# Transposed scores for the first two attention tiles, in a fused attention, gated FFN and expert kernel

## Chip, cores and metric

One core of one Trainium2 chip runs the whole program. The metric is device time in microseconds (us) of one execution; 788.37 us is the median of three runs of the kernel before (788.2 to 789.08).

## What is computed

Three stages follow each other: windowed attention, a gated FFN, and a mixture of eight experts with one expert per token. Cut to what matters here:

```python
scores = scale * np.matmul(q, k.transpose(0, 1, 3, 2))       # 4 x 8 heads, 576 tokens, 64 wide
mask = (rel >= 0) & (rel < 64)
scores = np.where(mask, scores, -1000000000.0)
scores = scores - np.max(scores, axis=-1, keepdims=True)
attn = np.exp(scores)
attn = attn / (np.sum(attn, axis=-1, keepdims=True) + 1e-09)
x = np.matmul(attn, v)
xn = x / np.sqrt(np.mean(x * x, axis=-1, keepdims=True) + 1e-06) * rms_g
g = xn @ w_gate
x = (g * (1.0 / (1.0 + np.exp(-g))) * (xn @ w_val)) @ w_out
out[token] = gate * eom * (np.maximum(x @ w1[e], 0.0) @ w2[e])   # e = argmax of x @ gate
```

The 2304 tokens are 18 tiles of 128. The FFN is 512 to 1536 and back, the experts 512 to 1024 and back. Large products are made of three single-pass products of split operands (high with high, high with low, low with high).

## The kernel before

**Attention of a tile** is `attention_tile` (L667 to L888). Two PSUM banks hold the scores of four heads each. `mmc` forms them: four bf16 matmuls write the mask (L691), 24 f32 matmuls of 64 rows and 64 columns of the array add the products (L699). VectorE takes the largest value of a row (`mx`, L743), ScalarE scales it (`mxs`, L775) and makes the exponentials with four instructions for four heads (`ex`, L782), each with its own bias and its own row sum. TensorE transposes the probabilities (`pt`, L796), VectorE or ScalarE copies them out of PSUM (L454, L458), and TensorE multiplies them with the values (`pv`, L830). Then come the division by the sum (`guard` L810, `rc` L815, `xr` L464), the squares (L843), the norm (L848, L853, L856), a transposition (`turn`, L873) and the split into high and low parts (L454, L461).

**FFN** (`ffn_group`, `ffn_step`): for each of 12 slices of the hidden layer, 12 matmuls for the gate and 12 for the value (`gv`, L1033 to L1035), then 12 back (`mo`, L1074 to L1076). Four tiles make the first group, and its first `gv` needs all four. The weights of each slice are brought from 64 to 32 bits and split on VectorE and ScalarE during the first group. Routing (L1142, L1149, L1157), scattering and the experts (L1508 to L1741) follow.

**A branch that is already there.** With `t < K["st"]` (`turned_too`), a tile takes another way, which the kernel before never takes since `st` is 0 there. `mmt_` forms the scores a second time with keys and queries exchanged, so transposed, beside `mmc`. `less` adds the negated largest value to every column with a matmul whose stationary operand is that value spread over 128 columns and whose moving operand is the identity. One exponential over four heads writes the transposed probabilities, and `total_` makes the row sums with matmuls by a vector of ones (the lines are those of the kernel before, one more in the changed one):

```python
# L750 to L765
for i in range(4):
    nc.tensor.matmul(
        bt.t[:, i * P:(i + 1) * P], lhsT=mb.t[:, 4 * hf + i:4 * hf + i + 1].to_broadcast([P, P]),
        rhs=ident.t, start=False, stop=(i == 3),
    )
...
nc.scalar.activation(out=pb.t, in_=bt.t.rearrange("p (i t) -> p i t", t=P), func=AF.Exp, scale=scale)
...
nc.tensor.matmul(sm.t[:, at:at + 2], lhsT=pb.t[:, i], rhs=ones.t, start=True, stop=True)
...
pl.op({"t": 0.9}, less, r=[(mb, hf), ident], w=[bt], prio=ps_, rows=0.5)
pl.op({"a": 0.55}, ext, r=[bt], w=[pb], prio=ps_)
pl.op({"t": 0.45}, total_, r=[pb, ones], w=[(sm, hf)], prio=pr + 5 * sg + 0.1 * hf, rows=0.05)
```

All of these are f32 and stand once per half of a tile; `mmt_` (L714 and L724) stands once per tile.

**What sets the order.** Nothing is issued in the order of the source. `Plan.order` goes through all operations before the program is built, with a cost for each on each engine (as the 0.45 above, in us), a due time, and a correction of that due time from the table `SHIFT`. It gives each operation an engine, a place in that engine's order, and the buffer that is free first by its own reckoning. The numbers in `K` set due times, buffer counts and such. Where it sees TensorE without work in the beginning, `filled` puts in pairs of bf16 matmuls that no one reads (`fill`, L625), up to the time `K["warm"]`. Each engine then runs its instructions strictly in that order, and waits where an operand or a buffer is not ready. All loads are on SyncE's queue (SP): queries, keys and values at L660, weights at L898.

Of the kernel before, what the change touches and what calls it, by code (L numbers as in the profile page):

```python
# [35 lines left out]
TICK, FULL = 3.4133, 1.275  # L36
LAT = {"t": 0.17, "a": 0.15, "v": 0.15, "p": 0.12, "s": 0.2}
K = dict(
    w_r=4, sl=1.2, n_q=4, n_kt=4, n_s=4, n_m=4, n_p=4, n_x=4, n_xf=1, n_val=3, pf=0.1, cold=6.0, late=1, f0=24.0, pw=110.0, pb=0.6, c1a=0, c1v=0, st=0, lact=0, warm=51.238, wf=21.971, flead=24.233, nwv=1, port=1.0, t0=46.214, pp=93.267,
    lead=1.781, clead=9.978, stag=2.552, stage=1.001, slack=0.083, nt=2, look=0.033, marg=-0.474, dw=1.368, ewl=3.278,  # L40
    ews=8.339, xld=43.407, xtn=7.222, mlead=14.712, vb=0.137, vb2=0.687, tb=30.293, share=-0.016, pls=9, phs=9, sf=0, hfs=1.431, stk=-0.032, rlead=7.936, span=0.317, wl=1.841,
)


SHIFT = [
# [40 lines left out]
]  # L86


class Buf:


    def __init__(self, tag=None, t=None, like=None):
        self.tag, self.t, self.slot, self.like = tag, t, None, like
        self.last_w, self.reads = {}, {}
        self.users = 0
        self.left, self.end = 0, 0.0
        self.before = None
# [1819 lines left out]
```

## Time and profile before

| | |
|---|---|
| median of 3 runs | 788.37 us |
| the profiled execution | 788.36 us, its span 786.6 us |
| TensorE busy | 778.0 us (99%), 5712 matmul records |
| VectorE, ScalarE busy | 394.1 us (50%), 349.5 us (44%) |
| mean granted TensorE clock | 0.998 |
| DMA | 135 MB, mean 172 GB/s |

Matmuls overlap in the pipeline. So a matmul's own duration is longer than what it adds to the time; what it adds is read from the start of one group of rows to the start of the next. An f32 matmul that isn't a transposition or a split product leaves two records. "Idle before" an instruction is time in which its engine did nothing, and the arrow names what ended it.

### The profile page before, as it was taken

The numbers are of one execution on the slowest core, as the hardware profiler recorded it, in microseconds if no ns is written. First come the engines' busy times: TensorE is split into PE (matmuls) and PEld (weight loads), VectorE is DVE, ScalarE is ACT, GpSimd is POOL, SyncE is SP. The second block draws the span as 40 slices with busy tenths as digits, with TensorE's granted clock in tenths as the row PEclk, the third lists the DMA queues.
The fourth block names the chain that finished last, engine by engine and source line by source line (L and its number), as shares of the span: only waits on it lengthen the run. The fifth ranks groups of instructions, "written<-read, shape, count | busy, mean of one in ns | idle before, by whom it ended". The sixth has DMA issues, their size and how long they took to land.

```text
span 786.6 us, 14688 instructions
## 1 busy us (share of the span) xinstructions
PE 778.0 (99%) x5712; PEld 663.8 (84%) x5712; DVE 394.1 (50%) x915; ACT 349.5 (44%) x938; POOL 56.0 (7%) x108
## 2 busy tenths in 40 slices
PE   8999999999999999999999999999999999999996
PEld 7988888888888888888888888899989998999883
DVE  5988988464323226332253422258445656656500
ACT  6988788472213335411351211424344553554411
POOL 1000000002000002000002000020100011111010
PEclk9999999999999999999999999999999999999999
DMA  7888898965421027231024740274194466675511
GB/s 259 291 293 307 280 330 279 302 215 184 147 108 68 28 108 229 81 111 51 1 108 161 267 161 0 102 261 148 49 323 169 140 201 212 174 257 188 182 32 69
DMA packets 51131, 135.17 MB, mean 172 GB/s; under 512 B 6052, under 2 KB 6052, under 8 KB 51060
## 3 DMA queue, kind: packets, MB, share of 16 engines
q1 hardware_dynamic: 48052, 124.68, 47.0%
q0 software_dynamic: 3008, 9.54, 3.2%
q8 instruction: 45, 0.74, 0.4%
q14 instruction: 26, 0.21, 0.1%
HBM read 109.97 MB, written 24.23 MB: 171 GB/s over the span
## 4 chain that ended last, share of the span: by engine, by line
PE 95%; issue 3%; DMA 1%; POOLq 0%; SPq 0%; POOL 0%; ACT 0%; DVE 0%
PE bank L1033 13%; PE bank L1035 13%; PE bank L1034 13%; PE bank L1074 6%; PE bank L1075 6%; PE bank L1076 6%; PE bank L1578 4%; PE bank L1579 4%; PE bank L1580 4%; PE bank L1739 3%; PE bank L1740 3%; PE bank L1741 3%; PE bank L830 2%; PE bank L796 2%; PE bank L699 2%
## 5 line engine op out<-in xcount | busy, mean ns | idle before, releaser
L1033 PE MATMUL bank<-xn,w 128*128 128x512 f32 (+1 forms) x480 | 181.3, 378 | 0.0
L1035 PE MATMUL bank<-xn,w 128*128 128x512 f32 (+1 forms) x480 | 177.0, 369 | 0.0
L1034 PE MATMUL bank<-xn,w 128*128 128x512 f32 (+1 forms) x480 | 176.8, 368 | 0.0
L1033 PEld LDWEIGHTS bank<-xn,w 128*128 128x128 f32 x480 | 90.3, 188 | 15.7 <-PE bank L1149 0.4
L1035 PEld LDWEIGHTS bank<-xn,w 128*128 128x128 f32 x480 | 90.2, 188 | 15.7
L1034 PEld LDWEIGHTS bank<-xn,w 128*128 128x128 f32 x480 | 90.5, 189 | 14.4
L1050 DVE SCALAR_TENSOR_TENSOR u<-u,bank 128x512 f32<-128x512 f32 (+1 forms) x60 | 37.9, 632 | 115.4 <-ACT u L1045 115.3
L1074 PE MATMUL bank<-wo,h 128*128 128x512 f32 x216 | 85.3, 395 | 0.0
L1075 PE MATMUL bank<-wo,h 128*128 128x512 f32 x216 | 84.2, 390 | 0.0
L1076 PE MATMUL bank<-wo,h 128*128 128x512 f32 x216 | 84.2, 390 | 0.0
L1045 ACT ACTIVATE u<-bank 128x512 f32<-128x512 f32 (+1 forms) x60 | 33.4, 556 | 102.1 <-PE bank L1035 99.0
L461 DVE TENSOR_TENSOR w<-raw,w 128x512 fp32r<-128x512 f32 x112 | 72.0, 687 | 5.9 <-ACT w L454 5.5
L454 ACT CAST h<-u 128x512 fp32r<-128x512 f32 (+1 forms) x54 | 31.0, 574 | 93.5 <-DVE u L1058 93.5
L1058 DVE TENSOR_TENSOR u<-u,bank 128x512 f32<-128x512 f32 (+1 forms) x60 | 38.0, 633 | 65.6 <-PE bank L1035 61.4
L454 ACT CAST w<-raw 128x512 fp32r<-128x512 f32 x86 | 49.1, 621 | 23.2 <-PE bank L1741 8.7
L1578 PE MATMUL bank<-xT,w 128*128 128x240 f32 (+4 forms) x192 | 58.2, 303 | 0.0
L1579 PE MATMUL bank<-xT,w 128*128 128x240 f32 (+4 forms) x192 | 57.7, 300 | 0.0
L1580 PE MATMUL bank<-xT,w 128*128 128x240 f32 (+4 forms) x192 | 57.7, 300 | 0.0
L782 ACT ACTIVATE s<-bank,m 128x128 f32<-128x128 f32 x144 | 50.7, 369 | 0.6
L461 DVE TENSOR_TENSOR h<-u,h 128x512 fp32r<-128x512 f32 (+1 forms) x60 | 38.2, 636 | 21.8 <-ACT h L454 21.5
L1589 DVE SCALAR_TENSOR_TENSOR eh<-bank,eh 128x240 fp32r<-128x240 f32 (+5 forms) x56 | 25.4, 459 | 46.4 <-ACT eh L1584 46.3
L1076 PEld LDWEIGHTS bank<-wo,h 128*128 128x128 f32 x216 | 40.6, 188 | 8.7
(235 smaller groups left out, 1308.2 us busy)
## 6 DMA issues: line engine op xcount, KB each, us to landing
w<-whd SPq DMA_DIRECT2D x64, 512.0 KB, 4.2
raw<-in_moe_w_dram SPq DMA_DIRECT2D x64, 512.0 KB, 4.5
whd<-w SPq DMA_DIRECT2D x24, 512.0 KB, 6.4
val<-in_v_dram SPq DMA_DIRECT2D x18, 512.0 KB, 6.7
raw<-in_moe_w_gate_dram SPq DMA_DIRECT2D x12, 512.0 KB, 4.6
raw<-in_moe_w_val_dram SPq DMA_DIRECT2D x12, 512.0 KB, 5.3
raw<-in_moe_w_out_dram SPq DMA_DIRECT2D x12, 512.0 KB, 4.7
q<-in_q_dram SPq DMA_DIRECT2D x18, 256.0 KB, 6.2
```

Source lines behind the costliest of these rows:

```text
L454: nc.scalar.copy(o, i)
L461: ve[e].tensor_tensor(out=o, in0=i, in1=h, op=ALU.subtract)
L782: nc.scalar.activation(out=s.t[:, h], in_=score()[:, h], func=AF.Exp, bias=mb.t[:, at:at + 1], scale=scale, accum_out=mb.t[:, 8 + at:9 + at],)
L1033: nc.tensor.matmul(o, lhsT=h_, rhs=xn.t[:, 0, kk], start=(kk == 0), stop=False)
L1034: nc.tensor.matmul(o, lhsT=h_, rhs=xn.t[:, 1, kk], start=False, stop=False)
L1035: nc.tensor.matmul(o, lhsT=l_, rhs=xn.t[:, 0, kk], start=False, stop=(kk == KD - 1))
L1074: nc.tensor.matmul(o.t, lhsT=h.t[:, 0, c], rhs=wo.t[:, 0, f], start=begin, stop=False)
L1075: nc.tensor.matmul(o.t, lhsT=h.t[:, 0, c], rhs=wo.t[:, 1, f], start=False, stop=False)
L1076: nc.tensor.matmul(o.t, lhsT=h.t[:, 1, c], rhs=wo.t[:, 0, f], start=False, stop=end)
L1578: nc.tensor.matmul(o, lhsT=wh, rhs=x.t[:, 0, kk, 0:N], start=(kk == 0), stop=False)
L1579: nc.tensor.matmul(o, lhsT=wh, rhs=x.t[:, 1, kk, 0:N], start=False, stop=False)
L1580: nc.tensor.matmul(o, lhsT=wl, rhs=x.t[:, 0, kk, 0:N], start=False, stop=(kk == KD - 1))
```

## The change

`st` becomes 2, so the first two tiles take the branch above. Their 16 transpositions of probabilities, 16 exponentials and four copies out of PSUM are left out; 16 mask matmuls, 64 f32 score matmuls, 16 matmuls of `less`, 16 of `total_` and four exponentials are put in. Other numbers of the planner change too, and `SHIFT` is a new table of 966 numbers (960 before), so that the whole program has a new order:

```diff
-    w_r=4, sl=1.2, n_q=4, n_kt=4, n_s=4, n_m=4, n_p=4, n_x=4, n_xf=1, n_val=3, pf=0.1, cold=6.0, late=1, f0=24.0, pw=110.0, pb=0.6, c1a=0, c1v=0, st=0, lact=0, warm=51.238, wf=21.971, flead=24.233, nwv=1, port=1.0, t0=46.214, pp=93.267,
-    lead=1.781, clead=9.978, stag=2.552, stage=1.001, slack=0.083, nt=2, look=0.033, marg=-0.474, dw=1.368, ewl=3.278,
-    ews=8.339, xld=43.407, xtn=7.222, mlead=14.712, vb=0.137, vb2=0.687, tb=30.293, share=-0.016, pls=9, phs=9, sf=0, hfs=1.431, stk=-0.032, rlead=7.936, span=0.317, wl=1.841,
+    w_r=4, sl=1.2, n_q=4, n_kt=4, n_s=2, n_m=4, n_p=4, n_x=3, n_xf=1, n_val=3, pf=0.1, cold=6.0, late=1, f0=24.0, pw=110.0, pb=0.6, c1a=0, c1v=0, st=2, lact=0, warm=71.25, wf=1.748, flead=24.233, nwv=1, port=1.0, t0=46.214, pp=93.267,
+    lead=1.781, clead=9.978, stag=2.552, stage=1.001, slack=0.136, nt=2, look=-0.01, marg=0.053, dw=1.465, ewl=3.278,
+    ews=8.339, xld=43.407, xtn=7.222, mlead=14.712, vb=0.239, vb2=1.813, tb=128.137, share=-0.093, pls=9, phs=9, sf=0, hfs=1.431, stk=53.771, rlead=7.936, span=0.317, wl=1.841,
...
 SHIFT = [
-    -19.2, -24.5, -5.2, 0.4, 19.1, -18.4, 11.5, -41.3, -36.1, -77.7, -50, -39.7, -49.9, -45.8, -43.9, 9.4, -30.1, -89.9, -41.7, -38.3, -26.1, -43.7, -22.4, -19.6,
...
+    0.8, 34.8, 45.4, 40.4, 10.4, 22.9, -1, -6, -30.1, -51, -44.2, -16.5, -6.6, 8.8, 2.6, -13.9, 10.6, -16, -0.3, 27.5, 0.8, -7.6, -32.3, 17.1,
...
```

`stk` lets an operation that uses a quarter of the array (`mmc`, `mmt_`, L1149) go ahead of others when one has just run, and `wf` and `warm` say how many fills are put in and until when. Of fills there are 238 matmuls before and 148 after; the first 34 are the same.

Three places of the new order matter for what follows. The first is the start of SyncE's queue, which loads queries (`q`), keys (`kt`) and values (`val`), each tile's in turn. Before:

```order
L660 DMA q_178<-in_q_dram 128x512
L660 DMA kt_202<-in_k_dram 128x512
L660 DMA val_231<-in_v_dram 128x1024
L660 DMA q_271<-in_q_dram 128x512
L660 DMA kt_311<-in_k_dram 128x512
L660 DMA kt_313<-in_k_dram 128x512
L660 DMA q_315<-in_q_dram 128x512
```

After:

```order
L661 DMA q_178<-in_q_dram 128x512
L661 DMA kt_199<-in_k_dram 128x512
L661 DMA val_229<-in_v_dram 128x1024
L661 DMA val_269<-in_v_dram 128x1024
L661 DMA kt_311<-in_k_dram 128x512
L661 DMA q_313<-in_q_dram 128x512
L661 DMA q_359<-in_q_dram 128x512
L661 DMA kt_366<-in_k_dram 128x512
```

The values of the second tile have moved ahead of its keys and queries, and its queries now come behind its keys.

The second is TensorE after the scores of the first three tiles (`bank_490` has the sums of the first tile, `bank_411` and `bank_412` the transposed scores of the second, `bank_516` the first tile's attention; `s_458` and `s_459` are the third tile's probabilities). After:

```order
L765 MATMUL bank_490<-ones,p_282 128x2 x4
L765 MATMUL bank_490<-ones,p_281 128x2 x4
L754 MATMUL bank_411<-ident,m_453 128x128 x4
L831 MATMUL bank_516<-val_229,p_281 64x64 x2
...
L754 MATMUL bank_412<-ident,m_453 128x128 x4
L797 MATMUL bank_548<-ident,s_458 128x128 x4
L765 MATMUL bank_554<-ones,p_377 128x2 x4
...
L797 MATMUL bank_566<-ident,s_459 128x128 x4
```

Before, the first tile's two transpositions (L796, from `s_281` and `s_282`) stood there, with 28 fills around them, and its `pv` came behind the scores of the third tile.

The third is ScalarE over the same stretch (`m_357`, `m_497`: small values of the first and third tile; `p_281`, `p_282`, `p_377`, `p_378`: transposed probabilities). Before:

```order
L775 ACTIVATE m_321<-m_321 128x4
L782 ACTIVATE s_281,m_321<-bank_279,m_321 128x128 x4
L782 ACTIVATE s_282,m_321<-bank_280,m_321 128x128 x4
L454 COPY p_399<-bank_398 128x512
L782 ACTIVATE s_353,m_394<-bank_351,m_394 128x128 x4
L782 ACTIVATE s_354,m_394<-bank_352,m_394 128x128 x4
```

After:

```order
L760 ACTIVATE p_281<-bank_315 128x512
L760 ACTIVATE p_282<-bank_316 128x512
L776 ACTIVATE m_497<-m_497 128x4
L811 ACTIVATE m_357<-bank_490 128x8
L783 ACTIVATE s_458,m_497<-bank_456,m_497 128x128 x4
L760 ACTIVATE p_377<-bank_411 128x512
L783 ACTIVATE s_459,m_497<-bank_457,m_497 128x128 x4
```

The third tile's exponentials now stand behind `guard` of the first tile (L811), which reads the sums that `total_` makes on TensorE.

## Rows read from the trace of the kernel before

**Rows 1.** The page: busy time of the engines, and the chain that ended last.
```profile
PE 778.0 (99%) x5712; PEld 663.8 (84%) x5712; DVE 394.1 (50%) x915; ACT 349.5 (44%) x938; POOL 56.0 (7%) x108
...
PE 95%; issue 3%; DMA 1%; POOLq 0%; SPq 0%; POOL 0%; ACT 0%; DVE 0%
```

**Rows 2.** Windows: busy us (instructions) by engine, granted clock, DMA share, GB/s.
```profile
5.00:10.00 5.00, 3.97 (x111) 3.27 (x113) 1.46 (x3) 2.84 (x16) 0.00 (x0) 1.00 0.98 338
10.00:15.00 5.00, 5.00 (x142) 4.62 (x135) 3.00 (x8) 3.71 (x19) 0.00 (x0) 1.00 0.90 340
100.00:140.00 40.00, 40.00 (x259) 32.90 (x258) 35.01 (x65) 33.00 (x76) 0.55 (x1) 1.00 0.89 307
500.00:600.00 100.00, 99.98 (x688) 89.87 (x687) 55.48 (x192) 38.66 (x93) 9.20 (x14) 1.00 0.54 185
```

**Rows 3.** Timeline of TensorE, first 11 us: start, us, instruction, [idle before].
```profile
1.40 3.70 PE L625 MATMUL warm<-ones_b 128*128 128x128 bf16 x34 [1.40 <-DVE ones_b L537]
5.03 0.41 PE L691 MATMUL bank<-masks,both_b 64*64 64x512 bf16 x4
5.27 1.09 PE L699 MATMUL bank<-kt,q 64*64 64x64 f32 x48
6.30 1.51 PE L625 MATMUL warm<-ones_b 128*128 128x128 bf16 x24
7.74 0.41 PE L691 MATMUL bank<-masks,both_b 64*64 64x512 bf16 x4
8.87 0.33 PE L699 MATMUL bank<-kt,q 64*64 64x64 f32 x4 [0.71 <-DMA q<-in_q_dram]
9.51 1.09 PE L699 MATMUL bank<-kt,q 64*64 64x128 f32 x44 [0.31 <-DMA kt<-in_k_dram]
```

**Rows 4.** Line L625, the fills: duration ns, first and last start.
```profile
L625 PE MATMUL warm<-ones_b x238: 216/219/314, 1.4 to 35.2; 128*128 128x128 bf16 x119
```

**Rows 5.** Timeline of TensorE, the last fills and the first FFN matmul.
```profile
29.77 3.07 PE L625 MATMUL warm<-ones_b 128*128 128x128 bf16 x52
32.68 0.61 PE L873 MATMUL bank<-ident,x 128*128 128x128 f32 x4
...
35.21 0.48 PE L1033 MATMUL bank<-xn,w 128*128 128x512 f32 x1
```

**Rows 6.** Timeline of TensorE, 167 to 170 us, with a matmul of 16 moving columns.
```profile
167.12 0.66 PE L796 MATMUL bank<-ident,s 128*128 128x128 f32 x4
167.61 0.52 PE L1157 MATMUL bank<-pick,lgt 128*128 128x16 f32 x4
168.06 0.41 PE L691 MATMUL bank<-masks,both_b 64*64 64x512 bf16 x4
168.30 1.09 PE L699 MATMUL bank<-kt,q 64*64 64x64 f32 x48
169.32 0.50 PE L1033 MATMUL bank<-xn,w 128*128 128x512 f32 x1
169.66 0.40 PE L1034 MATMUL bank<-xn,w 128*128 128x512 f32 x1
169.89 0.40 PE L1035 MATMUL bank<-xn,w 128*128 128x512 f32 x1
```

**Rows 7.** Groups by line, 755 to 772 us: the full-array f32 matmul of the plain expert.
```profile
L1675 PE MATMUL bank<-xw,raw 128*128 128x168 f32 x64 | 9.3, 306 | 0.0
```

**Rows 8.** Timeline of TensorE, 51 to 53 us: one `pv`.
```profile
51.42 1.15 PE L830 MATMUL bank<-val,p 128*64 128x64 f32 x32
52.50 0.50 PE L1074 MATMUL bank<-wo,h 128*128 128x512 f32 x1
```

**Rows 9.** Timeline of VectorE and ScalarE: maxima and exponentials of the first tile.
```profile
6.40 1.29 DVE L743 TENSOR_REDUCE m<-bank 128x4 f32<-128x512 f32 x2 [3.80 <-PE bank L699]
...
7.36 0.37 ACT L782 ACTIVATE s<-bank,m 128x128 f32<-128x128 f32 x1
...
8.75 0.38 ACT L782 ACTIVATE s<-bank,m 128x128 f32<-128x128 f32 x1
```

**Rows 10.** The page, costliest groups: an activation of 128x512 out of PSUM.
```profile
L1045 ACT ACTIVATE u<-bank 128x512 f32<-128x512 f32 (+1 forms) x60 | 33.4, 556 | 102.1 <-PE bank L1035 99.0
```

79 rows, old and new, of the table SHIFT are left out of this document.

## The prediction, made blind

> **What bounds the kernel now.** I read the page first: TensorE is busy 99% of the span, and the chain that ended last runs 95% on it [rows 1]. Busy time counts overlapping matmuls and could hide a stall, so I went on to the windows. From 10 us to the end of the FFN, TensorE is busy through each whole stretch, while VectorE and ScalarE, at 35 and 33 us of 40 in the fullest one, still keep up [rows 2]. The timeline of the start shows the only waits of some size: TensorE begins at 1.40, and the second tile's scores wait for queries and keys [rows 3]. Everything else until 35.21, where the FFN starts, is attention work with fills between [rows 4, 5].
>
> So the time is what TensorE has to execute, plus what it waits in the first 10 us, plus a tail that the change leaves alone. Work taken from VectorE and ScalarE is worth nothing by itself. It pays only by letting the plan leave out fills, which are the one thing on TensorE that is not needed. The question is whether the fills that go weigh more than the matmuls that come.
>
> **Fills.** 238 become 148, and the first 34 are the same, so 90 go from the stretch at the full clock. There 52 take 2.91 us from their start to the next group's [rows 5], 0.056 each. That is -5.0 us.
>
> **Second scores.** A tile's `mmc` takes 1.27 us from its first mask matmul to the next group [rows 3]. `mmt_` streams the same number of columns through each quarter of the array: 8 times 256 mask columns against 4 times 512, and per quarter 512 f32 columns in both. It stands directly behind `mmc`, so some 0.07 us of changing over falls away: 1.2 us a tile, 2.4 for both. Bounds are 1.0 (the matmuls of L699 alone) and 1.4, if the 64 records cost as much each as the 48 of `mmc`.
>
> **Largest value by TensorE.** `less` has 8 f32 matmuls a tile, 16 records, on the full array. The nearest rows are four records of L1157 in 0.45 us, so 0.11 each, with 16 moving columns [rows 6], and 64 records with 168 moving columns in 9.3 us, 0.145 each [rows 7]. With 128 columns it lies between; scaled by columns, the second gives 0.111. I take 0.11: 1.76 a tile, 3.5 for both, at most 4.6 at the upper row.
>
> **Sums by ones.** `total_` has 8 matmuls a tile too, each with a new 128x128 f32 stationary operand and only 2 moving columns. L1157 is nearest: 16 moving columns, and still 0.11 us a record, as much as a transposition with 128 [rows 6]. So the time doesn't follow the moving columns there, and 2 will not be cheaper: 16 records, 1.76 a tile, 3.5 for both. The plan reckons 0.45 for each of four groups that these rows put at 0.88, so fills behind the sums stand where TensorE has no gap left. The lowest price in the rows for a f32 record with a new stationary operand is `pv`, 32 in 1.08 us, 0.034 [rows 8], though there two halves of the array work side by side; it would make 1.1 for both tiles.
>
> The Trainium skill's page "TensorE: Matmul & The Clock Gate", section "Back-to-back issue gap", gives about 60 cycles or 25 ns for matmuls of 1 to 64 columns, which would make the sums 0.8 us instead of 3.5 and the time 2.7 us lower. L1157 has a number that the trace sets against it, 0.11 us, and I go by that.
>
> **Transpositions left out.** 16 of them, 8 a tile; four take 0.49 us with the change-over into the next group [rows 6], so 0.12, and 0.11 without it: -1.8.
>
> **Changing over.** The first full-array matmul behind `mmc` ends at 169.82, 0.43 after the last of `mmc` (169.39), where its successors follow at 0.23 to 0.24 [rows 6]: leaving `mmc` costs 0.2 us. `pv` is alike: it ends at 52.57, the next matmul at 53.00, 0.43 again [rows 8]. Along the two orders, a group of `mmc`, `mmt_`, `pv` or L1149 is followed by full-array work 38 times before and 32 times after, mostly since `mmc` runs into `pv` six times instead of two. Six times 0.2 is -1.2. The number of entries is all but the same (46 and 45).
>
> **The wait for the second tile's loads.** Before, its masks start at 7.74, its scores could end 0.24 + 1.09 later at 9.07, and end at 10.60 [rows 3]: 1.5 us lost. Its queries, fourth in the queue, arrive by 8.87, its keys, fifth, by 9.51: 0.64 us for 256 KB. After, 512 KB of values go ahead (two times 0.64): keys at 10.15, queries at 10.79. TensorE gets there at 6.30 + 1.2 (`mmt_`) + 0.2 (change) + 1.76 (`less`) = 9.46; VectorE has both maxima at 7.69 [rows 9], so `less` isn't held. Masks end at 9.70, and the scores start at 10.79: 1.1 us lost. Difference -0.4, between -1.5 (loads in time) and +0.5 (one more load behind).
>
> **What lies beside.** Eight exponentials of a tile, 1.39 us for four [rows 9], become two of about 0.56 [rows 10]; copies out of PSUM go as well. This is cover, not path: worth 0.
>
> **Sum.** -5.0 + 2.4 + 3.5 + 3.5 - 1.8 - 1.2 - 0.4 = +1.0 us. The profiled execution took 788.36 (span 786.6 and 1.8 around it), the median of the runs is 788.37, so both bases agree: **789.4 us**, +0.13%. Within 0.2% (1.6 us) is about what a measurement of this kernel can't tell from no change, so this is no change, on the slow side of it.
>
> **Rivals.**
>
> *The sums are cheap.* If 2 moving columns cost what a `pv` record does, 2.4 us go: 787.0. By the page's 25 ns it would be 786.7. For it: the plan's own cost is half of mine. Against it: L1157, which shows no gain from 16 columns over 128. Where it holds, ScalarE becomes the next to be late, which gives part of it back. 20%.
>
> *ScalarE holds TensorE* (slower). Its order puts the third tile's exponentials behind `guard` of the first, and that behind the sums. Worked on from above: second tile's scores done at 11.9, its `mmt_` at 13.1, third tile's scores 14.4, sums 16.3; `guard` 16.5; exponentials of the third tile until 17.9, one transposed 18.5, the other half 19.9. TensorE meanwhile: `less` 17.2, `pv` 18.3, `less` 19.4, then the third tile's first transposition, sums 20.7, fills, the second transposition at 20.9. Slack is 1.5 and 1.0 us. If the third tile's loads or ScalarE are over 1 us later than that, TensorE waits, and the four tiles before the first `gv` pass the wait on. With 2 us of it: 791.4. For it: only four fills stand in this stretch to take it up. Against it: fills of 32 and 44 matmuls stand later, and the sums, slower than planned, give ScalarE time. 20%.
>
> *The clock falls* (slower). Granted clock is 1.00 in every window from 5 us on [rows 2]; the first 34 fills, at 0.107 each, ran at the lower of its two levels (1.2 GHz), later ones at 0.056 at 2.4 [rows 3, 5]. Before, fills stand between all groups up to 13 us; after, none do between 5 and 20.7, and sums and `less` take their place. If the clock is taken back there, `less` and `pv` of the second tile and the third tile's scores (1.76 + 1.1 + 1.27) take twice as long: +4, or 793.5. The Trainium skill's page "TensorE: Matmul & The Clock Gate", section "Part 1: The HAM clock gate", says that the default state is throttled and that activity releases it; the first 5 us agree. Against it: TensorE is not idle there beyond the one wait of 1.1 us, and a wait of 1.0 us did not lower it before. 6%.
>
> The remaining 54% are the forecast, with small waits or savings of the new order that no row shows.
>
> **How the numbers follow.** The forecast (54%) has a range of its own of 787.9 to 790.9: the bounds of the loads and of `mmt_`, and half a us either way for the new order. The limits of no change are 786.8 and 789.9, so of it 0.04 lie below, 0.34 within and 0.16 above. Cheap sums (20%) lie at the lower limit: 0.14 faster, since the new order may add to it, and 0.06 within. A ScalarE hold (20%) is slower in 0.15 and too small in 0.05; the clock (6%) is slower. Faster 0.18, same 0.45, slower 0.37. The range reaches from the cheap sums, 786.8, to a hold of two us, 791.6; the clock, longer holds and the far end of cheap sums stay out.
>
> **What would show it.** Right: in the profile after, `total_` and `less` at 0.11 us a record; 148 fills; the second tile's scores waiting until about 10.8 for queries; no idle TensorE between 12 and 780; the first `gv` at some 41 us instead of 35.2, with six tiles' scores done by then instead of five; leaving `mmc` fewer times. Wrong: records of `total_` at half of that or less; idle time of TensorE put down to ScalarE between 16 and 40 us; a granted clock below 1.00 in a window; or an FFN stretch where TensorE waits for weights.

## The result, and the profile after

The changed kernel takes 798.59 us, the median of four runs (796.96 to 800.4); the kernel before, beside it on the same chip, 788.29. The ratio is 1.0135 [1.0119, 1.0152]: 10.3 us slower, and outside the predicted range of 786.8 to 791.6. The profiled execution took 796.96 us, its span is 795.2 us, 8.6 more than the span before.

The page of the changed kernel, busy time of the engines, the queue that fetches instructions, and the chain that ended last (compare [rows 1]):

```profile
PE 783.3 (99%) x5814; PEld 669.5 (84%) x5814; DVE 380.1 (48%) x881; ACT 360.4 (45%) x936; POOL 55.6 (7%) x108
...
q8 instruction: 46, 0.75, 0.4%
...
PE 92%; issue 4%; DMA 2%; POOLq 0%; SPq 0%; ACT 0%; DVE 0%; POOL 0%
```

TensorE is busy 99%, as before, which shows how little that share says. The waits of TensorE (what it waited for: us in total, times, longest) say more:

```profile
PE bank L765 <- issue: 2.8, 1, 2.8
PE warm L626 <- DVE ones_b L538: 1.4, 1, 1.4
PE bank L700 <- issue: 0.7, 1, 0.7
PE bank L700 <- DMA q<-in_q_dram: 0.5, 1, 0.5
```

Only the second and the last are expected ones. Two have no engine, buffer or load behind them, only "issue", and they are new. In the timeline of TensorE (start, us, instruction, [idle before]) they stand here:

```profile
5.81 0.43 PE L715 MATMUL bank<-both_b,masks 64*64 64x256 bf16 x8
6.03 1.15 PE L725 MATMUL bank<-q,kt 64*64 64x64 f32 x64
7.10 2.05 PE L754 MATMUL bank<-ident,m 128*128 128x128 f32 x16
9.08 0.41 PE L692 MATMUL bank<-masks,both_b 64*64 64x512 bf16 x4
9.95 1.10 PE L700 MATMUL bank<-kt,q 64*64 64x64 f32 x45 [0.45 <-DMA q<-in_q_dram]
11.75 0.27 PE L700 MATMUL bank<-kt,q 64*64 64x64 f32 x2 [0.70 <-issue]
...
14.30 0.27 PE L765 MATMUL bank<-ones,p 128*128 128x2 f32 x1
17.40 3.03 PE L765 MATMUL bank<-ones,p 128*128 128x2 f32 x15 [2.83 <-issue]
20.29 2.06 PE L754 MATMUL bank<-ident,m 128*128 128x128 f32 x8
22.28 1.98 PE L831 MATMUL bank<-val,p 128*64 128x64 f32 x32
24.18 1.36 PE L754 MATMUL bank<-ident,m 128*128 128x128 f32 x8
25.38 0.60 PE L797 MATMUL bank<-ident,s 128*128 128x128 f32 x4
```

TensorE stops in the middle of the second tile's scores, and again after the first record of the sums. The sums had their operands: the exponentials that they read had ended by 9.8 us. The windows (busy us and instructions of PE, PEld, DVE, ACT and POOL, granted clock, DMA share, GB/s; before: [rows 2]) show a second loss behind the longer stop:

```profile
10.00:15.00 5.00, 3.88 (x173) 3.54 (x173) 1.92 (x4) 0.00 (x0) 0.00 (x0) 1.00 1.03 367
15.00:20.00 5.00, 2.60 (x14) 2.60 (x14) 0.66 (x2) 0.20 (x1) 0.00 (x0) 0.78 0.25 98
20.00:25.00 5.00, 5.00 (x48) 4.66 (x48) 0.93 (x3) 3.56 (x18) 0.00 (x0) 0.54 0.00 0
25.00:30.00 5.00, 5.00 (x119) 4.75 (x120) 3.86 (x11) 3.68 (x9) 0.68 (x1) 1.00 0.65 214
```

The granted clock is 1.00 throughout the stop (14.57 to 17.40), fell from the upper level (2.4 GHz) to the lower (1.2 GHz) at 17.8 us, just after TensorE had gone on, and came back at 24.6. The first `gv` starts at 46.53 instead of 35.21 [rows 5].

**What the stops have in common.** Counting all of TensorE's records from the first (5814 weight loads, 5814 matmuls and 110 of its sequencer, semaphores above all), the two stops stand before the 450th and the 706th: 256 apart. The queue of kind "instruction" in the page moved 46 packets of together 0.75 MB, 16 KB each, and 11,738 such records make 46 times 255: one packet brings about 256 instructions of TensorE. The DMA view of three neighbouring windows, 9.4 to 10.5, 10.5 to 15 and 15 to 16.2 us (queue, kind: packets, MB, share of 16 engines), shows when the two packets went:

```profile
q1 hardware_dynamic: 231, 0.42, 100.7%
q8 instruction: 1, 0.02, 5.7%
...
q1 hardware_dynamic: 598, 1.64, 102.6%
...
q1 hardware_dynamic: 101, 0.35, 71.3%
q8 instruction: 1, 0.02, 5.5%
```

By the packets' own records they ran from 9.45 to 10.45 and from 15.07 to 16.12; TensorE went on at 11.75 and 17.40, 1.3 us behind each. The second packet began 3.3 us after TensorE had taken up its 450th instruction, while the loads filled the DMA engines. And this was the change's doing: the 256 records from the 450th to the 706th took 2.8 us up to the stop at 14.57, where before they took 4.4 (13.66 to 18.08). Scores on quarters of the array, plain and transposed, back to back, use them up fastest here: 72 matmul records of `mmt_`, each with its weight load, in 1.3 us. In the kernel before, the same packet landed at 16.57 and the 706th record ran at 18.08. Taking the same 1.3 us after the landing, that is about 0.2 us short of a stop (an estimate).

The Trainium skill's page "Runtime: NRT & Kernel Launch", section "Instruction fetch mechanics", says that instruction memory is refilled in 16 KiB blocks of 256 instructions by a queue of the sequencer, while the block at hand runs. The packets here agree. It also calls the cost of crossing a block "mostly hidden"; here 2.83 us of it were not.

### The profile page after: what moved, and what is told of

Read it like the earlier page. It is cut to its first block, busy times and chain, and to the rows that moved or that the text cites. A ratio compares the mean times of both kernels' runs of the same rounds, so it can differ in the third digit from the quotient of the medians.

```text
span 795.2 us, 14881 instructions
## 1 busy us (share of the span) xinstructions
PE 783.3 (99%) x5814; PEld 669.5 (84%) x5814; DVE 380.1 (48%) x881; ACT 360.4 (45%) x936; POOL 55.6 (7%) x108
## 4 chain that ended last, share of the span: by engine, by line
PE 92%; issue 4%; DMA 2%; POOLq 0%; SPq 0%; ACT 0%; DVE 0%; POOL 0%
PE bank L1034 13%; PE bank L1036 12%; PE bank L1035 12%; PE bank L1075 6%; PE bank L1076 6%; PE bank L1077 6%; PE bank L1579 4%; PE bank L1581 3%; PE bank L1580 3%; PE bank L831 3%; PE bank L1740 2%; PE bank L1742 2%; PE bank L1741 2%; PE bank L700 2%; PE bank L797 2%
## 5 line engine op out<-in xcount | busy, mean ns | idle before, releaser
L455 ACT CAST h<-u 128x512 fp32r<-128x512 f32 (+1 forms) x59 | 34.0, 576 | 88.2 <-DVE u L1059 88.2
L455 ACT CAST w<-raw 128x512 fp32r<-128x512 f32 x112 | 63.5, 618 | 17.1 <-DMA raw<-in_moe_w_dram 7.0
L1077 PEld LDWEIGHTS bank<-wo,h 128*128 128x128 f32 x216 | 40.5, 188 | 8.7
L1075 PEld LDWEIGHTS bank<-wo,h 128*128 128x128 f32 x216 | 40.6, 188 | 8.2
L1076 PEld LDWEIGHTS bank<-wo,h 128*128 128x128 f32 x216 | 40.6, 188 | 7.7
```

The source lines that it names most:

```text
L455: nc.scalar.copy(o, i)
L1075: nc.tensor.matmul(o.t, lhsT=h.t[:, 0, c], rhs=wo.t[:, 0, f], start=begin, stop=False)
L1076: nc.tensor.matmul(o.t, lhsT=h.t[:, 0, c], rhs=wo.t[:, 1, f], start=False, stop=False)
L1077: nc.tensor.matmul(o.t, lhsT=h.t[:, 1, c], rhs=wo.t[:, 0, f], start=False, stop=end)
```

## The experiments

Three theories went into the first four runs. *Instructions*: TensorE stops where the next block of 256 has not landed. *Data*: the stops are a load or buffer that the trace does not name. *Clock*: the narrow matmuls of the sums themselves let the clock fall. Later runs ask what the rest of the loss is, and what fills are worth. All times are medians, with the ratio to the kernel before on the same chip (its medians: 787.98 to 788.82).

**1. Fewer instructions at the start** (the first 12 fill matmuls of the changed kernel left out).

```diff
+    early = [o for o in seq if o.seq == -1][:6]
+    seq = [o for o in seq if o not in early]
```

> The changed kernel with 12 of the first 34 fills left out, so 24 TensorE instructions (12 weight loads, 12 matmuls) fewer at the very start; all else in the same order. Theory F (TensorE runs out of instructions, which are fetched in blocks of 256): the two waits without a releaser stand before the 450th and the 706th TensorE record again, whatever these are, so 24 instructions later in the program: the second one not behind the first matmul of the sums but behind about the 13th. Theory D (they are waits for data or a buffer that the profile doesn't name): both stay at the same instructions of the program, the second behind the first matmul of the sums. Time in both 796 to 801.

795.21 us in one run. The timeline of TensorE in this run:

```profile
11.82 1.10 PE L725 MATMUL bank<-q,kt 64*64 64x64 f32 x60 [0.75 <-issue]
...
14.04 1.61 PE L765 MATMUL bank<-ones,p 128*128 128x2 f32 x13
17.74 0.66 PE L765 MATMUL bank<-ones,p 128*128 128x2 f32 x3 [2.09 <-issue]
```

The stops moved to other instructions, into the second `mmt_` and behind 13 records of the sums, and stand again before the 450th and the 706th record. A late operand would have stayed with its instruction. So the instruction theory holds here and the data theory falls.

**2. Less load traffic at the start** (two weight loads held back on SyncE's queue).

```diff
+    held_back, behind = sp[12:14], sp[14]
...
+    at = seq.index(behind) + 1
+    seq[at:at] = held_back
```

> The changed kernel with the loads of the first two weight slices (1 MB) moved in SyncE's queue behind the values of the fourth tile, which wait for the first tile's pv. Theory F: the DMA engines run dry some 2 us earlier, the fetch that began at 15.07 begins earlier (13 to 14), the wait of 2.8 us before the sums shrinks to 0.5 to 1.8, and the granted clock stays nearer to 1.00 between 15 and 25 us: 790 to 796. The weights come later, which could give some of it back. Theory D: wait and time as in the changed kernel, 796 to 801, or longer.

799.35 us, 1.0125 [1.0106, 1.0144]. The second packet now began 1.1 us after the 450th record instead of 3.3, at 13.84, and the stop before the sums shrank from 2.83 to 0.9:

```profile
PE bank L1509 <- DMA t2k<-xs: 2.2, 1, 2.2
PE bank L874 <- DVE x L857: 1.4, 1, 1.4
...
PE bank L700 <- issue: 1.1, 1, 1.1
PE bank L765 <- issue: 0.9, 1, 0.9
PE bank L831 <- issue: 0.5, 1, 0.5
```

The stop answers to the traffic, as the instruction theory has it, but the time did not follow. The wait for VectorE is new, and behind it the clock fell to 0.66 from 30 to 35 us. New as well is the wait of 2.2 us for a load in the experts, at 583.6 us, with the lower clock for 3.4 us behind it. What brought it is not shown (experiment 1 has 0.7 us of the same wait), and the profiled execution is the slowest of the four (800.61). More than the stop moved, so this run says nothing on what the stop is worth.

**3. Work in place of the stop** (12 bf16 matmuls of 512 columns, which nobody reads, ahead of the second `mmt_`).

```diff
+    at = [n for n, o in enumerate(seq) if getattr(o.fn, "__name__", "") == "mmt_"][1]
+    seq[at:at] = [wide_op() for _ in range(12)]
```

> The changed kernel with 12 bf16 matmuls of 512 columns that no one reads (2.6 us at the full clock, 24 instructions) put in front of the second tile's transposed scores, shortly before the wait of 2.8 us. If the clock fell because TensorE stood still (theory F, with the clock as its consequence): the wait shrinks by about what was put in, the granted clock stays at 1.00 from 15 to 25 us, and the time falls by 2 to 4 us, to 793 to 797, though work was added. Theory C (the clock falls by itself over the narrow sums and the largest-value matmuls): granted clock still about 0.5 to 0.8 there, time 797 to 801.

796.8 us, 1.0101 [1.0084, 1.0118]: 2.7 us of work more than the changed kernel and about 2 us less time (1.8 by the two medians, 2.3 when each is set against the kernel before on its chip). The timeline of TensorE:

```profile
12.88 2.76 PE L1866 MATMUL warm<-ones_b 128*128 128x512 bf16 x12
...
17.99 1.95 PE L765 MATMUL bank<-ones,p 128*128 128x2 f32 x16
19.80 1.14 PE L754 MATMUL bank<-ident,m 128*128 128x128 f32 x8
20.87 1.15 PE L831 MATMUL bank<-val,p 128*64 128x64 f32 x32
```

and two of its windows:

```profile
15.00:20.00 5.00, 5.00 (x146) 4.38 (x144) 1.29 (x2) 0.23 (x2) 0.00 (x0) 1.00 0.25 97
20.00:25.00 5.00, 5.00 (x71) 4.80 (x71) 2.35 (x8) 4.53 (x21) 0.00 (x0) 1.00 0.27 101
```

The long stop is gone and the clock stays at 1.00, through the same sums. So the sums do not lower the clock by themselves. The wide matmuls put in ahead of them might have held it up, but experiment 7 has nothing put in, and there too it stays at 1.00 through the same sums, where the stops are shorter. So the clock theory falls. The sums take 1.81 us for 16 records, 0.113 each, and TensorE waits for ScalarE nowhere.

**4. More instructions, without the change** (in the kernel before, the fills from the 18th pair to the 80th have half the columns and twice the number).

```diff
-        for _ in range(2):
-            nc.tensor.matmul((bank.t if bank else warm[0])[:, 0:P], lhsT=ones_b.t, rhs=ones_b.t, start=True, stop=True)
+        for _ in range(2 if len(made_fills) <= 17 or len(made_fills) > 80 else 4):
+            n = P if len(made_fills) <= 17 or len(made_fills) > 80 else 64
...
```

> The kernel before, without transposed scores, whose fills after the first 34 and up to 126 are 64 columns wide instead of 128 and twice as many: the same columns with twice the instructions. Theory F: waits without a releaser appear before the 706th and perhaps the 450th and 962nd TensorE record, 0.5 to 3 us in all, and the time is 1 to 6 us above the kernel before. Theory D, or one in which only the new matmuls wait: no such wait, time within 0.2% of before, or longer by the fills alone if a narrow one costs as much as a wide one (at most 5 us, without waits).

790.78 us, 1.0028 [1.0017, 1.0039]. TensorE's waits have `PE warm L627 <- issue: 0.7, 1, 0.7`, and it stands before record 1218, which is 450 and three times 256. Instructions alone make the stop, with no transposed score in the program. It is shorter than in the changed kernel, and it stands at none of the three records that the expectation had named. One more idle stretch put down to "issue", 0.4 us at 307.8 us, stands before record 5697, which is no such place; it stays unexplained.

**5. The transposed scores on the plan of the kernel before** (its `K` and `SHIFT`, with `st=2`, `n_s=3` and `n_x=3`, entries repeated for the new operations).

```diff
-    ... n_s=2, ... n_x=3, ... st=2, ... warm=71.25, wf=1.748, ...
+    ... n_s=3, ... n_x=3, ... st=2, ... warm=51.238, wf=21.971, ...
...
```

> The transposed scores for the first two tiles on the plan of the kernel before (its table of numbers and its due times, entries repeated for the added operations). The first tile's scores, transposed scores and largest values still use up TensorE's instructions within the first 20 us. By the instruction theory: unnamed waits (put down to 'issue') of 0.5 to 3 us in front of about the 450th or 706th record counted from the start, and a time of 791 to 799 us. By the rival that the new plan alone makes the kernel slow (its load order or its order on ScalarE): no unnamed wait over 0.3 us, and a time below 791 us.

807.56 us, 1.0238 [1.0221, 1.0255]. There is one stop of 0.5 us, before record 450 again; none at 706. `pv` and half of the sums of the first tile now lie between the second tile's scores and its transposed ones, so the 256 records take 4.3 us instead of 2.8, and the packet began 1.2 us after record 450 instead of 3.3. The time went elsewhere: 12.4 us of the difference between the profiled executions (spans 808.2 and 786.6) are in the FFN, where TensorE waits for VectorE:

```profile
PE bank L1038 <- DVE u L1055: 3.2, 2, 2.8
PE bank L1038 <- DVE u L1063: 2.7, 1, 2.7
PE bank L1081 <- DVE h L466: 1.9, 1, 1.9
```

Neither theory had that. The old table probably does not fit the shifted operations; that is not shown. At the full clock the second scores take 2.4 us here, `less` 4.0 and the sums 3.7.

**6. The new plan without the transposed scores** (`st=0`, with `K` and `SHIFT` of the changed kernel otherwise).

```diff
-    ... n_s=2, ... n_x=3, ... st=2, ... warm=71.25, ...
+    ... n_s=2, ... n_x=3, ... st=0, ... warm=71.25, ...
```

> The new plan without the transposed scores (the first two tiles take the old way again). 64 matmuls on quarters of the array and the narrow sums are gone. By the instruction theory: no unnamed wait over 0.5 us in the first 20 us and a granted clock of 1.00 from 10 us on; the time is that of the new order alone, 787 to 793 us. By the rival that the new order is what stalls TensorE: the waits of 0.7 and 2.8 us stay and the time is 794 us or more.

799.5 us, 1.0139 [1.0114, 1.0163], outside the 787 to 793 of the instruction theory. The stops at 450 and 706 are gone and the clock is 1.00 throughout, as that theory had it; one of 0.9 us stands before record 1474. But `warm` lasts until 71.25 in this plan, and with the transposed scores gone the planner filled the room: 410 fill matmuls, 26.2 us of them. Without the scores the 256 records from 450 to 706 take 6.4 us, and a packet as late as in the changed kernel (3.4 us after record 450) holds nothing up. That fits the instruction theory, but the plan changed around it too, so the run does not show it alone, and it shows nothing on the plan's worth.

**7. The same fill columns in fewer instructions** (each pair of 128 columns as one of 256, the first 16 pairs as 8 of 512).

```diff
+        n = 2
+        if not bank and len(made_fills) <= 16:
+            if len(made_fills) % 2:
+                return
+            n = 4
+        nc.tensor.matmul(
+            (bank.t if bank else warm[0])[:, 0:n * P].rearrange("p (a b) -> p a b", b=P), lhsT=ones_b.t,
+            rhs=ones_b.t.unsqueeze(1).to_broadcast([P, n, P]), start=True, stop=True,
+        )
```

> The changed kernel with the same columns of fills in fewer instructions: the first 32 fill matmuls of 128 columns as 8 of 512, each later pair of 128 as one of 256. By the instruction theory the 450th record lies later in the program (some 45 instructions later or more), the stalls meet other work and are shorter; 794 to 798 us, 0.5 to 3 us below the changed kernel. By the rivals (load order, the sums' clock): within 1 us of the changed kernel, waits unmoved.

792.77 us, 1.0055 [1.0038, 1.0072]: 5.8 us below the changed kernel, more than expected. TensorE's waits (L733 is `mmt_` here, L839 `pv`):

```profile
PE bank L733 <- issue: 1.8, 1, 1.8
...
PE bank L839 <- issue: 0.4, 1, 0.4
```

The stops are again before records 450 and 706, and 1.3 us shorter together. The clock stayed at 1.00 in every window; two of them:

```profile
10.00:15.00 5.00, 3.17 (x152) 2.96 (x155) 1.29 (x2) 0.60 (x1) 0.00 (x0) 1.00 1.04 356
15.00:20.00 5.00, 4.63 (x91) 4.31 (x82) 1.53 (x4) 2.58 (x14) 0.00 (x0) 1.00 0.29 116
```

So the sums, and `less` and `pv` of the second tile, ran at full speed. The two profiled executions lie 4.1 us apart (spans 795.2 and 791.1): 1.3 are the stops, and most of the rest is the clock. The expectation had only the stop in it, not what the stop does to the clock.

**8. The changed kernel without the later fills** (114 matmuls, 6.4 us).

```diff
+    late = [o for o in seq if o.seq == -1][17:]
+    seq = [o for o in seq if o not in late]
```

> The changed kernel without the fills that stand after the first 34 matmuls (114 matmuls of 128 columns left out; nobody reads them). If TensorE is late from the stalls on, all of these are pure loss: 64 to 114 of them at 0.056 to 0.1 us make 791 to 795 us. If they stand in true gaps, or if the clock falls further without them: no change or slower, 797 us or more. The unnamed waits stay either way, before other instructions than in the changed kernel if fills stand before them.

799.58 us, 1.0126 [1.01, 1.0153]: nothing gained.

```profile
PE bank L765 <- issue: 3.4, 1, 3.4
PE bank L797 <- DVE x L857: 1.9, 1, 1.9
...
PE bank L797 <- ACT s L783: 1.0, 1, 1.0
```

With the fills gone, TensorE waits for VectorE and ScalarE for 3 us in their place, the longer stop grows by 0.5, and the clock falls further:

```profile
15.00:20.00 5.00, 1.63 (x20) 1.47 (x10) 1.29 (x2) 0.21 (x1) 0.00 (x0) 0.75 0.33 131
20.00:25.00 5.00, 5.00 (x37) 4.78 (x38) 0.24 (x2) 2.44 (x13) 0.00 (x0) 0.50 0.01 3
...
40.00:45.00 5.00, 3.60 (x19) 2.71 (x20) 4.65 (x12) 4.84 (x18) 0.99 (x1) 0.64 1.02 340
```

The windows behind these two stretches have 0.72 (25 to 30 us) and 0.68 (45 to 50). I had taken the fills behind a stop for loss. Some of them stood in true gaps, and some kept the clock up; how the 6.4 us divide between the two is not shown.

**9 to 11. Fills, by halves.** In the kernel before, every second pair of fills behind the first 62 is left out, or all behind the first 34; in the kernel of experiment 7, every second of the later ones.

```diff
+    late = [o for o in seq if o.seq == -1][31::2]
+    seq = [o for o in seq if o not in late]
```

([17:] and [17::2] in the other two.)

> The kernel before without every second pair of the fills that stand behind its first 62 (88 of 238 fill matmuls left out, 88 at 0.056 us = 4.9 us of TensorE's work; nobody reads them). If the fills of the kernel before stand only in true gaps, as those of the changed kernel proved to do, the time stays within 1 us of 788.3. If TensorE is late behind them, up to 4.9 us go: 784 to 787. Third: gaps that lower the clock, 790 or more.

785.67 us, 0.9972 [0.9961, 0.9982]: **2.3 us faster than before**, and so faster than both kernels. The first `gv` starts at 32.74 instead of 35.21. TensorE now has small waits, and the clock stays at 1.00:

```profile
PE bank L873 <- DVE x L856: 1.2, 1, 1.2
...
PE bank L1033 <- DVE xn L461: 0.2, 1, 0.2
```

> The kernel before without any fill behind its first 34 (204 matmuls left out, 11.4 us of TensorE's work). If all stand in true gaps: idle time put down to ScalarE and VectorE of some 11 us, no gain, and a granted clock below 1.00 somewhere before 36 us, 789 to 794. If they are partly loss: 780 to 787.

787.99 us, 1.0002 [0.9992, 1.0011]: the first `gv` is earlier still, at 32.20, but the FFN starts at the lower clock:

```profile
30.00:35.00 5.00, 3.97 (x15) 2.92 (x15) 4.57 (x9) 5.00 (x14) 0.00 (x0) 0.63 0.91 324
35.00:40.00 5.00, 5.00 (x17) 4.00 (x16) 3.53 (x8) 2.80 (x12) 0.00 (x0) 0.68 0.87 276
```

> The changed kernel with the wide fills (as in the run with fewer, wider fills, 792.8) and every second of the later ones left out. The instruction stalls of 1.8 and 0.4 us stay, since they lie before the first of the fills left out. If those stand in true gaps: 792 to 794. If TensorE is late behind the stalls: 789 to 791.

791.33 us, 1.0042 [1.0027, 1.0058]. TensorE has 29 fills of 256 columns less, at 0.11 each 3.2 us, and the time is 1.2 to 1.4 us below experiment 7. The two intervals overlap, and 0.5 us of it is in the stops, so this run does not show how much of the fills was loss. The new wait is `PE bank L805 <- ACT s L791: 0.9, 1, 0.9`. The stops, 1.1 and 0.6, stand before records 450 and 706 once more.

**All stops together.** Idle time of TensorE over 0.3 us in the first 50 us that is put down to "issue", in all profiled kernels, with the record counted from the first:

| kernel | stops: record (us) |
|---|---|
| before; half and no fills of it | none |
| changed | 450 (0.70), 706 (2.83) |
| 1, fewer at the start | 450 (0.75), 706 (2.09) |
| 2, less traffic | 450 (1.13), 706 (0.91), 1730 (0.54) |
| 3, work in place | 450 (1.11), 1730 (0.75) |
| 4, more fills in before | 1218 (0.67) |
| 5, old plan | 450 (0.47) |
| 6, without transposed scores | 1474 (0.95) |
| 7, wide fills | 450 (1.83), 706 (0.37) |
| 8, no later fills | 450 (0.70), 706 (3.37) |
| 11, half of the wide fills | 450 (1.07), 706 (0.64) |

Eighteen stops in ten programs, before matmuls of five kinds (scores, transposed scores, sums, `pv`, fills), and every one stands at record 450 or a multiple of 256 behind it. In all eighteen a packet of the instruction queue had landed 1.2 to 1.6 us before TensorE went on. That TensorE waits for a block of instructions is shown. Why a packet starts 0.4 us after its block is entered in one place (record 962 with half of the fills of before) and 4.4 in another (record 706 of the kernel before) is shown only as far as experiment 2 goes: one came sooner with less load traffic.

## Why the prediction was wrong

**The step that failed** is the second paragraph: "the time is what TensorE has to execute, plus what it waits in the first 10 us, plus a tail". It assumed that instructions are always at hand. With it fell the sign to look for, "no idle TensorE between 12 and 780", and the argument against the clock rival, "TensorE is not idle there beyond the one wait of 1.1 us". In its place the runs show 3.5 us in which TensorE waited for its own instructions, and 3.1 us of lower clock behind them. The first `gv`, forecast at some 41 us, came at 46.53; in experiment 7, with shorter stops and the clock up, it came at 41.80.

Adding up, over TensorE's records in order, what each ends later than the one before it, gives the ledger (us, change against the kernel before). The last column is experiment 3, whose clock stayed up, with its two stops and the 2.7 us of added work left out. The terms are rounded one by one. The ledger is that of the profiled execution, 8.6 us over the one before; the other 1.7 us of the medians' 10.3 have no trace.

| term | forecast | changed kernel | experiment 3 |
|---|---|---|---|
| fills | -5.0 | -5.7 | -5.3 |
| second scores | +2.4 | +2.3 | +2.4 |
| `less` | +3.5 | +5.2 | +4.1 |
| sums | +3.5 | +7.8 with the stop of 2.8 | +3.65 |
| transpositions | -1.8 | -2.6 | -2.6 |
| changing over (`gv`, `mo`, `pv`) | -1.2 | +0.2 | -0.1 |
| loads (`mmc`) | -0.4 | -0.7 without the stop of 0.7 | -0.7 |
| experts, L1157 and tail | 0 | +1.3 | +1.2 |
| others | 0 | +0.2 | +0.2 |
| sum | +1.0 | +8.6 with the stop of 0.7 | +2.9 |

- **Stops: 3.5 us, not foreseen.** Their risk could have been. The profile before has the instruction queue with 45 packets for its 11,543 records, so 256 to a packet, and in its first 50 us no 256 records in a row take less than 4.4 us. In the changed kernel the fastest 256 take 2.6. That a block comes too late for it, only the runs show.
- **Clock: 3.1 us, a rival at 6%.** The price was right (+4 forecast) and the work named was nearly right. In the changed kernel 15 records of sums take 2.89 us, two `less` 1.99 and 1.20, `pv` 1.90; in experiment 3 they take 1.70, 1.07, 0.99 and 1.08. The cause I gave, thin work in place of fills, was wrong (experiments 3 and 7): the clock fell behind the stop of 2.83 us.
- **Sums: right.** 0.113 us a record at the full clock, against 0.11 from L1157 [rows 6]. Two moving columns cost no less than 16, so the rival of cheap sums falls. On the page "TensorE: Matmul & The Clock Gate" (the Trainium skill, section "Back-to-back issue gap") the 25 ns are for a matmul by itself; the section says that such figures leave out the weight load. Here each matmul has a new f32 stationary operand, and a record takes 113 ns.
- **`less`: undersized.** 0.126 a record with experiment 3 (1.98 and 1.07 and 0.99 for 32) instead of 0.11: +0.5 us. It lies between the two rows that I had named, 0.11 and 0.145.
- **Second scores: right**, 2.3 to 2.4 for both tiles.
- **Fills: right in the sum** (148 of them, -5.7 against -5.0), but a fill left out did not gain its price: 2.3 of 4.9 us in experiment 9, next to nothing of 11.4 in experiment 10 and of 6.4 in experiment 8.
- **Transpositions and changing over.** The forecast was -3.0 for both. The transpositions gave 0.8 more than their own price and the groups behind `mmc` nothing: -2.7 together in experiment 3. Right as a sum, wrong in its place.
- **Loads.** Queries came at 9.95, not 10.79; TensorE waited 0.45 for them, not 1.1.
- **ScalarE holds TensorE** did not happen in the changed kernel, which waits for ScalarE nowhere. With fills left out, TensorE waits 1.0 and 0.9 us for exponentials (experiments 8 and 11), but for a later tile's, at 43.2 and 33.3 us, and not for the third tile's that the rival was about.
- **Not foreseen:** the experts take 0.7 us more, L1157 0.5, the tail 0.2. "A tail that the change leaves alone" did not hold for a program that was planned anew as a whole. Why was not tried.

Without the stops (3.5), the clock (3.1) and 0.4 of a later `pv` (at 45.05 us it takes 0.4 longer than others; experiment 3 has a stop there before record 1730), 1.6 of the 8.6 us are left; experiment 3 has 2.9 left, and experiment 7, 792.8 less its stops of 2.2, is 2.3 over before. So the sum of durations, +1.0, was too low by 0.6 to 1.9, most of it in `less` and the later stages. What it left out weighs more: 7 us.

## What to carry to other kernels

Where an engine runs many short instructions (matmuls on quarters of the array above all), count its instructions as well as their time: if 256 of them pass faster than the next block arrives, which took 5.7 us in the changed kernel and 6.2 in experiment 8, the engine stops, and the profile calls it only "issue". Fewer and wider instructions are worth more than their own time there, because the clock can fall behind a stop. Fillers that keep TensorE busy are worth testing by halves: in the kernel before, every second of the later ones out gained 2.3 us, all of the later ones out nothing.

## What the runs showed of the hardware that was not expected

- A block's packet ran about 1 us, and TensorE went on 1.3 us after it had landed (10.45 to 11.75, 16.12 to 17.40); over all eighteen stops it was 1.2 to 1.6 us.
- A stop of 2.83 us was followed by granted clocks of 0.78 and 0.54 in two windows, one of 2.09 us by 0.79 and 0.87 (experiment 1); one of 1.83 us left it at 1.00 (experiment 7). The length alone does not decide it: a wait of 1.42 us for VectorE was followed by 0.66 (experiment 2).
- In the kernel before, the packet for record 706 came about 0.2 us before it would have held TensorE (an estimate by the 1.3 us above): a tuned kernel can stand next to such an edge, and its profile shows no wait there.
